# Two middle token blocks turned by DMA, and query halves in the last block pair, in a two-layer spectral and attention kernel

## The chip, the cores and the metric

The kernel runs on one core of a Trainium2 chip. The metric is the device time of one launch in microseconds. The engines are named as in the profile: PE (matmul), ACT (ScalarE), DVE (VectorE), POOL (GpSimd) and SP, whose queue issues nearly all DMAs.

## The reference, cut

x is one sequence of 2048 tokens of 512 elements in bfloat16. Two layers follow each other. Each is a spectral mixing A (a 2-D FFT of the normalized x, multiplied by complex weights, and the inverse) and an attention B with 32 query heads of 16 elements that share one key and one value head, each added to x.

```
def _A_ref(x, w_r, w_i):
    X = rfft2(x, axes=(-2, -1)) * (w_r + 1j * w_i)
    return irfft2(X, s=(S, D), axes=(-2, -1))
def _B_ref(x, wq, wk, wv, wo):
    q, k, v = heads(x @ wq), x @ wk, x @ wv
    p = softmax(q @ k.T * Dh ** -0.5)
    return merge(p @ v) @ wo
x = x + _A_ref(_layernorm(x), w_r, w_i)
x = x + _B_ref(_layernorm(x), wq, wk, wv, wo)
# and both once more
```

## The kernel before, in words

**Tiles.** Token rows are kept as x_sb with four blocks t of four tiles r, 128 rows each. t is also the attention's query block (512 queries). The rows of one block lie with stride 4 in the sequence, so that the FFT over tokens splits into a radix-4 step (`radix4`, L66 to L76), matmuls with tables, and the same again on the way back.

**Stages of a layer.** The front: statistics (`bn`), a transpose of x (`tr_x` on PE, or `turn_x` by way of DRAM), a matmul with the cosine and sine table PH (`mm1`, L1162), scaling by the reciprocal deviation on ACT (`mm1_evac`, L1175), radix-4 on DVE. The middle: matmuls with the tables FT (`mid`), the multiplication by the weights on DVE (`filt`, L1233 to L1236). The back, one block t after the other: inverse matmuls (`inv`), radix-4, `y_mm`, the addition to x (`add_x`, L1317), statistics, `rstd` on ACT, `shift` (L1108) and `apply` (L1115) on DVE, which make the normalized rows xnt; these are transposed on PE (`tr_n`, L1323) and copied to xT (`trn_evac`, L1326, the tile named gx) by ACT or DVE. From xT come K (`k_mm`, L1340), V (`v_mm`, L1352) and Q (`qt_mm`, L1366).

**Attention.** There are 32 blocks b per layer: query block qb, group g of eight heads, and parity par. A block has 64 units of work, 16 key chunks for four heads. One unit is a score matmul of 32 rows (L1382), an exponential, and a matmul with V (L1404). The exponential is made either on ACT (two units at a time, L1387) or on DVE: one operation turns scores into bfloat16 bits (`p1`, L1394), and two additions of constants give two further phases (`phase`, L1398 on POOL or L1400 on DVE), whose mean approximates the exponential. A finished block is transposed out of PSUM (`evac`, L1411); every second block closes a pair: `recip`, `mul`, and a turn by way of DRAM (`norm_dma`), or, for the last pair of a layer, a DVE transpose (`norm`, L1431). Then come the projections (`proj`, L1447), the addition to x and the front of the next layer.

**The order.** Nothing is scheduled at run time. A planner in the kernel file (`Plan`) goes through a modelled time and emits instructions one by one; each engine then runs its own list in order, and waits on semaphores. The planner has a duration for each task, a latency between engines, PSUM slots (four banks b, two double banks sa), and for what goes by DMA an assumed delay: `TURN` (7000 ns) and `OUT_TURN` (25000 ns). SCRIPT is a string of positions at which the planner doesn't take its best choice but the second one, pauses PE, or gives the phase additions to the other engine. DVE units begin (`dve_on`) when V of all four blocks is there; up to then only ACT makes exponentials. Dummy matmuls keep PE's clock up.

```
    def turn_x(self, L, tiles):
        (t, r), _ = tiles
        way = self.way.tile([2 * P, D], BF, name="way")
        self.nc.sync.dma_start(out=way.rearrange("(r p) d -> p r d", r=2), in_=self.x[:, r:r + 2, t, :])
        self.turned(L, tiles, way)
```

Of the kernel before, what the change touches and what calls it, by code (L numbers as in the profile page):

```python
# [10 lines left out]
P = 128  # L11
# [7 lines left out]
NC = 4  # L19
# [70 lines left out]
def phase_weights():  # L90
# [4 lines left out]
RANKS = ((), ())  # L95
TURNS = ("PE", "ACT", "DVE", "POOL", "wait", "few", "heads", "phase")
SCRIPT = (
    "0ax00902q00k05h0hw0po0c807l04j03c00801i00a00p0740ay04w00p01v0vn01903p0790l900i01f0630fk00q01202z0ad09i01h07k0h8"
    "08t0ib00a02g04s0bp08300c02q05k05101200q02300s00903n0960b202107m0ac07h00e00e01e0dc03g0by04r0500bx0rl00g0q803f06u"
    "03d03s02t00a01c08001401711p01q05g00j0ex0iy00t01a03807p05t08200k07409503o00g00x00g03914a00804107x04k01m0310ix00s"  # L100
    "02400u0rv02g05707s09a08805q02o03u02206s0mg03l01k02o03u01t00c04w07401m01l01o09s0d90w50ak0240ng09e03407500p00w00c"
    "06o06d08t03h02l0650c81380aq04o04u01h03f00r08i0190dc0bh11p0ud0e404z02103c01l01n02502s05k09906903f01y00x016018083"
    "03h00y02w02l01x06j0hy00o00r0at01q00z00w05n06m0lt05e00c05k0fx0i00740200m40560fx0mh01i00h04402000d00x02j07102x00k"
    "0b201101l0fc04t06q00p01101y0ls00m04w00i05n01x00j00902803m00s03m02u00l01808y0ba0a50z80wa00s0hw08o02c0ml084")


def script():

    out, n = {}, 0
    for i in range(0, len(SCRIPT), 3):  # L110
        v = int(SCRIPT[i:i + 3], 36)
        n += v // 8
        out.setdefault(n, []).append(TURNS[v % 8])
    return out


class Task:
# [5 lines left out]
    def __init__(self, eng, dur, deps, fn, take=None, give=(), then=None, prio=-1, order=0, lazy=0.0, gap=0.0, parts=1, port=False, lock=False, cols=None):  # L123
        self.ways = {eng: dur} if isinstance(eng, str) else dict(zip(eng, dur))
        self.eng, self.deps, self.fn = next(iter(self.ways)), deps, fn
        self.dur = self.ways[self.eng]
        self.take, self.give, self.then = take, give, then
        self.port, self.lock = port, lock
        self.cols = self.dur * 512.0 / 220.0 if cols is None else cols
        self.prio, self.order, self.lazy, self.gap, self.parts, self.step = prio, order, lazy, gap, parts, 0  # L130
        self.end = self.slot = None


class Plan:
# [34 lines left out]
    OUT_TURN = 25000.0  # L169
# [3 lines left out]
    def __init__(self):  # L173
        self.t = {"PE": 0.0, "ACT": 0.0, "DVE": 0.0, "POOL": 0.0}
# [18 lines left out]
        self.ranks, self.base = None, 0  # L193

    def ranked(self, which):

        self.ranks, self.base = RANKS[which], self.n

    def add(self, *a, **kw):
# [3 lines left out]
        if self.ranks is not None and k.order < 30:  # L203
            i = k.seq - self.base
            if i < len(self.ranks):
                k.prio, k.order, k.lazy = -1, self.ranks[i] / 32, 0.0
# [17 lines left out]
    def step(self):  # L224
        while True:
# [13 lines left out]
            self.turns.discard(eng)  # L239
            return  # L240
# [36 lines left out]
    def bg_next(self, eng):  # L277
        best = None
        for k in self.bg[eng]:
            if any(d.end is None for d in k.deps):  # L280
                continue
            if eng == "ACT" and len(k.ways) > 1 and self.at is not None and self.at.dve_on:
                continue
# [106 lines left out]
    def usable(self, kind):  # L390
# [9 lines left out]
        else:  # L400
            sd, free = (sum(1 for x in self.use if x == y) for y in ("sd", None))
            if not free or sd >= 3 or not at.dve_on and (sd >= self.EARLY_SD or free < 2 or not at.begun or us[0][1] // 4 not in at.v_ready):
                return False
# [3 lines left out]
        return at.unit_ready(us[0]) is not None  # L407

# [87 lines left out]
    def fill(self, start, after):  # L496
# [3 lines left out]
        while self.activity(start) < warm:  # L500
# [8 lines left out]
            else:  # L509
                return  # L510
            if start - t0 < self.MM + (self.PE_SW if mode != after else 0.0) and self.activity(start) >= force:
                return
# [3 lines left out]
            self.t["PE"] = t0 + self.MM  # L516
            if fresh:
                self.bank[i] = t0 + self.MM
# [115 lines left out]
class Attn:  # L634


    def __init__(self, plan, em, layer):
        self.plan, self.em, self.layer = plan, em, layer
        self.blocks = [(qb, g, par) for qb in range(NQB) for g in range(4) for par in range(2)]
        nb = len(self.blocks)  # L640
        first = [(b, 4 * t + r) for t in range(4) for b in range(layer.NFIRST) for r in range(4)]
# [53 lines left out]
    def unit_ready(self, u):  # L695
        b, kc, h = u
        qb, g, par = self.blocks[b]
        if (g, qb) not in self.qt_ready or (kc // 4, par) not in self.k_ready:
            return None
        return max(self.qt_ready[(g, qb)], self.k_ready[(kc // 4, par)])  # L700
# [10 lines left out]
    def done(self, b, slot, end):  # L711
# [5 lines left out]
        self.evac[b] = self.evac_last = ev  # L717
        if par == 0:
            return
        tail = 0.0 if b >= len(self.blocks) - 2 else 5000.0  # L720
        rc = p.add("DVE", 260.0, [ev, self.evac[b - 1]], lambda k: em.recip(self, b), lazy=tail)
        mu = p.add("DVE", 600.0, [rc], lambda k: em.mul(self, b), lazy=tail, port=True)
        if b < len(self.blocks) - 2:
            no = Mark("DMA", None)

            def turned(k):
                em.norm_dma(self, b)
                no.end = k.end + p.OUT_TURN

            mu.then = turned  # L730
        else:
            no = p.add("DVE", 626.0, [mu], lambda k: em.norm(self, b), lazy=tail)
        self.evac[b] = no
        if g == 3:
            self.layer.close_rows(qb, [self.evac[8 * qb + 2 * i + 1] for i in range(4)])


class Layer:
# [9 lines left out]
    PUTC = True  # L748
    FIRST_PUT = (0,)
    BN = ((4,), (4,), (4,), (2, 2))  # L750
# [16 lines left out]
    def pieces(self, durs, deps, fn, order, lazy=0.0, lock=False):  # L767

        for i, d in enumerate(durs):
            deps = [self.plan.add("DVE", d, deps, lambda k, i=i: fn(i), order=order, lazy=lazy, port=True, lock=lock)]  # L770
        return deps[0]
# [90 lines left out]
    def add_back(self):  # L862
        p, em, at = self.plan, self.em, self.at
        left = [T]
        for t in range(T):
            o = 20 + 10 * t
            cs = []
            for b in range(2):
# [17 lines left out]
                cs.append(self.pieces((332.0, 332.0, 400.0, 400.0), es, lambda i, t=t, b=b: em.radix_v(self, t, b, i), o))  # L886
            w = 2 if t == 0 else R
            te = []
            for j in range(0, R, w):
                key, ks = ("b", t, j), []  # L890
                for i, r in enumerate(range(j, j + w)):
                    put = t in self.FIRST_PUT
                    n = 5 if put else 4
                    y = p.add("PE", 217.0 * n, cs, lambda k, s, t=t, r=r, n=n: em.y_mm(self, t, r, k.slot, s, n), parts=n, take="b",
# [12 lines left out]
                nb = p.add("DVE", 100.0, [rs], lambda k, key=key, w=w: em.shift(self, key, w), order=o + 3)  # L907
                for i, r in enumerate(range(j, j + w)):
                    self.stat[("b", t, r)] = (rs, key, i)
                for a in range(j, j + w, 2):  # L910
                    ap = [p.add("DVE", 323.0, [nb], lambda k, t=t, r=r: em.apply(self, t, r), order=o + 3) for r in (a, a + 1)]
# [30 lines left out]
    def close_rows(self, qb, deps):  # L942
        p, em, at = self.plan, self.em, self.at
        t = qb
        if not self.last and t == T - 1:
            p.ranked(1)
# [9 lines left out]
        for r in range(R):  # L956
            if t == T - 1:
                m = p.add("PE", 660.0, deps[:3] + [self.at.evac_last], lambda k, r=r: em.proj(at, t, r, k.slot, 0, 3), take="b",
                          prio=-2)
                if not self.last and self.PUTC:  # L960
# [14 lines left out]
        w = 2 if t == T - 1 else R  # L975
        for j in range(0, R, w):
            n.add_stats(("f", t, j), [(t, r) for r in range(j, j + w)], rows[j:j + w])
        rows = [r.x if hasattr(r, "put") else r for r in rows]
        for j in range(0, R, 2):
            n.add_front([(t, j), (t, j + 1)], rows[j:j + 2], 1, turned[j // 2] if t < T - 1 else None)  # L980
        if t == T - 1:
# [3 lines left out]
            p.ranks = None  # L985


class Emit:
# [117 lines left out]
    def shift(self, L, key, n):  # L1106
        mv, sb = L.sb[key]
        self.nc.vector.scalar_tensor_tensor(out=sb[:, 1, :], in0=mv[:, :, 0], scalar=-1.0, in1=sb[:, 0, :],  # L1108
                                            op0=ALU.mult, op1=ALU.mult)

    def apply(self, L, t, r):
        xn = self.pool.tile([P, 512], BF, name="xnt", tag="xnt", bufs=6)
        _, key, i = L.stat[("b", t, r)]
        sb = L.sb[key][1]
        self.nc.vector.tensor_scalar(out=xn, in0=self.x[:, r, t, :], scalar1=sb[:, 0, i:i + 1], scalar2=sb[:, 1, i:i + 1],  # L1115
                                     op0=ALU.mult, op1=ALU.add)
        L.xn[(t, r)] = xn

    def load_x(self, L):
        for t in range(T):  # L1120
# [8 lines left out]
    def turn_x(self, L, tiles):  # L1129

        (t, r), _ = tiles
        way = self.way.tile([2 * P, D], BF, name="way")
        self.nc.sync.dma_start(out=way.rearrange("(r p) d -> p r d", r=2), in_=self.x[:, r:r + 2, t, :])
        self.turned(L, tiles, way)

# [183 lines left out]
    def tr_n(self, L, t, j, slot, i):  # L1319
        ps = self.ps(slot).bitcast(BF).rearrange("p (c i x) -> p c i x", i=2, c=NC)  # L1320
        xn = L.xn.pop((t, j + i))
# [6 lines left out]
    def trn_evac(self, L, t, j, slot, eng):  # L1328
# [3 lines left out]
        ps = self.ps(slot).bitcast(BF).rearrange("p (c x) -> p c x", c=NC)  # L1332
        self.copy(eng, xT[t][:, :, j:j + 2, :].rearrange("p c i x -> p c (i x)"), ps)
# [42 lines left out]
    def scores(self, at, slot, us):  # L1376
        for j, (b, kc, h) in enumerate(us):
# [3 lines left out]
            o = self.ps(slot)[:, j, :] if slot[0] == "sa" else self.ps(slot)  # L1381
            self.nc.tensor.matmul(o, lhsT=KX[rs, kc * P:(kc + 1) * P], rhs=at.QT[qb][rs, g, :], start=True, stop=True,  # L1382
# [24 lines left out]
    def evac(self, at, b, slot):  # L1407
        qb, g, par = at.blocks[b]
        if par == 0:
            at.raw[(qb, g)] = self.pool.tile([P, 2, 16, 32], F32, name="raw", tag="raw", bufs=3)  # L1410
        self.nc.vector.transpose(out=at.raw[(qb, g)][:, par].rearrange("p a b -> p (a b)"), in_=self.ps(slot))  # L1411

    def recip(self, at, b):
        qb, g, par = at.blocks[b]
        at.rc[(qb, g)] = self.small([2, 16], "rc", 2)
        self.nc.vector.reciprocal(out=at.rc[(qb, g)], in_=at.raw[(qb, g)][:, :, :, 16])

    def mul(self, at, b):
        qb, g, par = at.blocks[b]
        raw, rc = at.raw[(qb, g)], at.rc.pop((qb, g))  # L1420
# [5 lines left out]
    def norm(self, at, b):  # L1426
        qb, g, par = at.blocks[b]
        on = at.raw.pop((qb, g))
        if g == 0:
            at.OT[qb] = self.t4([4, 512])  # L1430
        self.nc.vector.transpose(out=at.OT[qb][:, g, :], in_=on.rearrange("p a h d -> p (a h d)"))  # L1431
# [24 lines left out]
def schedule(plan, em, n_pairs=2):  # L1456
# [5 lines left out]
    plan.ranked(0)  # L1462
    for t in range(T):
        arrive = Mark("DMA", 5500.0 + 2600.0 * t)
        tiles = [(t, r) for r in range(R)]
        j = 0
        for n in L.BN[t]:
            L.add_stats(("f", t, j), tiles[j:j + n], [arrive] * n)
            j += n
        for j in range(0, R, 2):  # L1470
            L.add_front(tiles[j:j + 2], [arrive], 1)
# [4 lines left out]
    plan.ranks = None  # L1476
# [61 lines left out]
```

The softmax here doesn't subtract the row's maximum and nothing guards it: scores larger than these inputs give would overflow.

## Time and profile before

| what | value |
|---|---|
| time, median of 3 runs | 1314.85 us (1314.13 to 1315.22) |
| the profiled execution | 1314.55 us, span 1312.7 us |
| DMA queue of SP and ACT | 108288 packets, 30.46 MB, 10.0% of the span |
| granted PE clock | 1.00 |
| ACT: one exponential of 128x1024 | 1.00 to 1.35 us |
| POOL: one phase addition | 1.04 us |

The page shows one execution. A busy time is the union of an engine's instructions; neighbours overlap by about a tenth of a microsecond, so that the spacing of two starts is a better price than the duration. The idle time in brackets in a timeline is that of the engine ahead of an instruction, with the instruction that ended it.

### The profile page before, as it was taken

What the parts mean: (1) busy time and instruction counts of PE and PEld (TensorE: products, weight loads), DVE (VectorE), ACT (ScalarE), POOL (GpSimd) and SP (SyncE); (2) the same over time, 40 slices, a digit from 0 to 9 for tenths busy, and PEclk for the clock granted to TensorE, in tenths of its full rate; (3) what the DMA queues carried; (4) which work ended last, traced back from release to release, by engine and by line L of the source; (5) the groups of instructions that cost most, each with busy time, mean ns of one, the idle gap of its engine ahead of it and who ended that gap; (6) DMA issues with size and microseconds to landing.
All of it is one profiled execution on the core that took longest, in us unless ns stands there. A gap on an engine that the chain in (4) does not pass through costs nothing.

```text
span 1312.7 us, 31767 instructions
## 1 busy us (share of the span) xinstructions
PE 1281.5 (98%) x12986; PEld 433.1 (33%) x12986; DVE 1272.7 (97%) x2277; ACT 1223.3 (93%) x1397; POOL 840.1 (64%) x825
## 2 busy tenths in 40 slices
PE   9999999999999999999999999999999999999997
PEld 5642222322232222222256423232222232233222
DVE  6999999999999999999979999999999999999998
ACT  6488999999999999999954899999999999999996
POOL 0005777767777677766720067787777777777775
PEclk9999999999999999999999999999999999999999
DMA  9100000011010100010051000000100010000101
GB/s 294 46 1 1 10 9 10 9 32 19 2 12 12 36 10 10 9 34 17 10 169 41 1 1 9 10 10 9 22 14 10 9 22 14 5 8 11 27 5 25
DMA packets 108722, 33.04 MB, mean 25 GB/s; under 512 B 88352, under 2 KB 107296, under 8 KB 108576
## 3 DMA queue, kind: packets, MB, share of 16 engines
q1 hardware_dynamic: 108288, 30.46, 10.0%
q8 instruction: 101, 1.65, 0.5%
q10 hardware_dynamic: 288, 0.56, 0.1%
q14 instruction: 45, 0.37, 0.1%
HBM read 17.89 MB, written 7.60 MB: 19 GB/s over the span
## 4 chain that ended last, share of the span: by engine, by line
ACT 72%; PE 18%; DVE 10%; issue 1%; DVEq 0%
ACT e_0_84 L1387 3%; ACT e_10_94 L1387 3%; ACT e_13_97 L1387 3%; ACT e_3_87 L1387 3%; ACT e_20_104 L1387 3%; ACT e_4_88 L1387 3%; ACT e_12_96 L1387 3%; ACT e_2_86 L1387 3%; ACT e_8_92 L1387 3%; ACT e_7_91 L1387 3%; ACT e_11_95 L1387 3%; ACT e_18_102 L1387 3%; ACT e_1_85 L1387 3%; ACT e_5_89 L1387 3%; ACT e_15_99 L1387 3%; ACT e_14_98 L1387 3%
## 5 line engine op out<-in xcount | busy, mean ns | idle before, releaser
L1382 PEld LDWEIGHTS <-KB 32*128 32x128 bf16 x2048 | 89.7, 91 | 228.5 <-issue 221.4
L1382 PEld LDWEIGHTS <-KA 32*128 32x128 bf16 x2048 | 86.4, 91 | 238.4 <-issue 231.5
L1404 PEld LDWEIGHTS <-vs_116 128*32 128x32 bf16 x2474 | 99.9, 94 | 93.0 <-issue 87.9
L1404 PEld LDWEIGHTS <-vs_117 128*32 128x32 bf16 x1622 | 96.0, 94 | 64.0 <-issue 60.5
L1404 PEld LDWEIGHTS <-vs_118 128*32 128x32 bf16 x1622 | 70.6, 94 | 70.5 <-issue 65.9
L1404 PEld LDWEIGHTS <-vs_119 128*32 128x32 bf16 x1622 | 68.4, 94 | 64.8 <-issue 61.4
L1398 POOL INT64_ADD w_1382<-w_1381 x1 | 1.0, 1040 | 108.1 <-DVE w_1381 L1394 108.1
L1398 POOL INT64_ADD w_10977<-w_10976 x1 | 1.0, 1038 | 97.2 <-DVE w_10976 L1394 97.2
L1387 ACT ACTIVATE e_6_90<-sa_64 128x1024 bf16<-128x1024 f32 x34 | 39.8, 1172 | 1.0 <-PE sa_65 L1382 1.0
L1091 DVE BATCH_NORM_STATS2 st<-x_sb 128x6 f32<-128x512 bf16 x52 | 35.4, 682 | 4.0 <-DMA x_sb<-in_A_x_dram 3.6
L1387 ACT ACTIVATE e_11_95<-sa_65 128x1024 bf16<-128x1024 f32 x31 | 36.5, 1178 | 0.7 <-PE sa_65 L1382 0.7
L1387 ACT ACTIVATE e_12_96<-sa_65 128x1024 bf16<-128x1024 f32 x31 | 36.9, 1189 | 0.2 <-PE sa_65 L1382 0.2
L1387 ACT ACTIVATE e_2_86<-sa_64 128x1024 bf16<-128x1024 f32 x31 | 36.5, 1178 | 0.4 <-PE sa_64 L1382 0.4
L1387 ACT ACTIVATE e_4_88<-sa_65 128x1024 bf16<-128x1024 f32 x31 | 36.6, 1182 | 0.1
L1387 ACT ACTIVATE e_1_85<-sa_64 128x1024 bf16<-128x1024 f32 x31 | 36.6, 1180 | 0.1
L1387 ACT ACTIVATE e_7_91<-sa_64 128x1024 bf16<-128x1024 f32 x31 | 36.6, 1181 | 0.0
L1387 ACT ACTIVATE e_15_99<-sa_65 128x1024 bf16<-128x1024 f32 x31 | 36.6, 1179 | 0.0
L1387 ACT ACTIVATE e_20_104<-sa_65 128x1024 bf16<-128x1024 f32 x31 | 36.4, 1175 | 0.0
L1387 ACT ACTIVATE e_13_97<-sa_64 128x1024 bf16<-128x1024 f32 x31 | 36.2, 1168 | 0.0
L1387 ACT ACTIVATE e_14_98<-sa_65 128x1024 bf16<-128x1024 f32 x31 | 36.0, 1162 | 0.0
L1387 ACT ACTIVATE e_0_84<-sa_65 128x1024 bf16<-128x1024 f32 x30 | 35.5, 1183 | 0.2 <-PE sa_65 L1382 0.2
L1387 ACT ACTIVATE e_9_93<-sa_64 128x1024 bf16<-128x1024 f32 x30 | 35.1, 1170 | 0.2 <-PE sa_64 L1382 0.2
(4077 smaller groups left out, 6474.8 us busy)
## 6 DMA issues: line engine op xcount, KB each, us to landing
it<-const_IT SPq DMA_DIRECT2D x8, 640.0 KB, 5.6
onw<-on SPq DMA_DIRECT2D x120, 32.0 KB, 1.9
x_sb<-in_A_x_dram SPq DMA_DIRECT2D x4, 512.0 KB, 6.8
out_dram<-x_sb SPq DMA_DIRECT2D x16, 128.0 KB, 1.9
way<-x_sb SPq DMA_DIRECT2D x6, 256.0 KB, 2.2
tab_PH<-const_PH ACTq DMA_DIRECT2D x1, 512.0 KB, 4.9
w_131<-const_FT SPq DMA_DIRECT2D x1, 512.0 KB, 8.8
w_136<-const_FT SPq DMA_DIRECT2D x1, 512.0 KB, 8.4
```

The lines of the kernel that those rows point to most:

```text
L1091: self.nc.vector.bn_stats(st, self.ps(slot) if slot else self.x[:, x[1], x[0], :])
L1382: self.nc.tensor.matmul(o, lhsT=KX[rs, kc * P:(kc + 1) * P], rhs=at.QT[qb][rs, g, :], start=True, stop=True, skip_group_check=True)
L1387: self.wrote("ACT", e, self.nc.scalar.activation(out=e, in_=self.ps(slot), func=ACT.Exp, scale=SCALE))
L1398: self.nc.gpsimd.int64_add(t[p][:, 0:n].bitcast(U64), t[0][:, 0:n].bitcast(U64), DELTA[p] * FOUR)
L1404: self.nc.tensor.matmul(self.ps(slot)[32 * h:32 * h + 32, :], lhsT=V[:, kc, :], rhs=rhs, start=first, stop=last, skip_group_check=True)
```

## The change

It does five things in one edit.

1. **Turn by DMA.** The normalized rows of the blocks t = 1 and 2 go to DRAM in two DMAs per pair of tiles, and come back by a DMA transpose into xT (`turn_n`). The transposes on PE and their evacuations fall away for these blocks. For t = 0 and 3 they stay, in the row order 0, 2, 1, 3.
2. **Query halves.** In each layer the last two blocks (b = 30 and 31) no longer stand for the two parities of 512 queries, but for the two halves of the queries, both parities each. Either half is closed by itself (`recip`, `mul`, `norm` at half size, then the projections of two row tiles).
3. **`shift` falls away**: `apply` subtracts the mean and multiplies by the reciprocal deviation. `y_mm` waits for the part of radix-4 that makes its row only.
4. **The start.** x of block 0 arrives in two DMAs, and the planner reckons with a slow PE clock in the first 4.4 us.
5. **The planner.** A new SCRIPT with one more kind of entry, `OUT_TURN` 9000 instead of 25000, the early close of the first half marked urgent.

```
+    DMA_T = (1, 2)
...
-    OUT_TURN = 25000.0
+    COLD = 4400.0
+    OUT_TURN = 9000.0
...
+        self.halves = {nb - 2: 0, nb - 1: 1}
...
+        if b in self.halves:
+            rc = p.add("DVE", 125.0, [ev], lambda k: em.recip(self, b))
+            mu = p.add("DVE", 335.0, [rc], lambda k: em.mul(self, b), port=True)
+            no = p.add("DVE", 340.0, [mu], lambda k: em.norm(self, b))
+            hf = self.halves[b]
+            self.layer.close_rows(qb, [self.evac[8 * qb + 2 * i + 1] for i in range(3)] + [no], (2 * hf, 2 * hf + 1))
+            return
...
-                nb = p.add("DVE", 100.0, [rs], lambda k, key=key, w=w: em.shift(self, key, w), order=o + 3)
...
+                for a in rows[::2]:
+                    d = 1 if t in self.DMA_T else 2
+                    ap = [p.add("DVE", 323.0, [rs], lambda k, t=t, r=r: em.apply(self, t, r), order=o + 3) for r in (a, a + d)]
+                    if d == 1:
+                        te.append(Mark("DMA", None))
+
+                        def applied(k, t=t, a=a, y=te[-1], ap=ap):
+                            if all(z.end is not None for z in ap):
+                                em.turn_n(self, t, a)
+                                y.end = k.end + p.TURN
+                        ap[0].then = ap[1].then = applied
+                        continue
...
+        for j in (0, 2):
+            self.nc.sync.dma_start(out=self.x[:, j:j + 2, 0], in_=self.xv[:, j:j + 2, 0])
+        for t in range(1, T):
...
+    def turn_n(self, L, t, a):
+
+        if t not in L.at.xT:
+            L.at.xT[t] = self.t4([NC, R, P], tag="gx", bufs=4)
+        way = self.way.tile([2 * P, D], BF, name="way", tag="way")
+        for i in range(2):
+            self.nc.sync.dma_start(out=way[P * i:P * i + P, :], in_=L.xn.pop((t, a + i)))
+        out = L.at.xT[t].rearrange("p c r x -> p c (r x)")[:, :, P * a:P * a + 2 * P]
+        self.nc.sync.dma_start_transpose(out=out, in_=way)
...
+            if b in at.halves:
+                q = 256 * at.halves[b]
+                for i, KX in enumerate((self.KA, self.KB)):
+                    self.nc.tensor.matmul(o[:, 256 * i:256 * i + 256], lhsT=KX[rs, kc * P:(kc + 1) * P],
+                                          rhs=at.QT[qb][rs, g, q:q + 256], start=True, stop=True, skip_group_check=True)
+                continue
```

The numbers of the exponentials made on ACT (1237) and of the p1 operations (1622) are the same in both programs. The phase additions on DVE grow from 3 to 9, those on POOL fall from 809 to 803.

## The prediction

> **What bounds the kernel now.** I read the page's busy shares first, then busy time by stage, then the timeline of VectorE (DVE) where a stage begins or ends.
>
> ```profile
> PE 1281.5 (98%) x12986; PEld 433.1 (33%) x12986; DVE 1272.7 (97%) x2277; ACT 1223.3 (93%) x1397; POOL 840.1 (64%) x825
> ```
>
> DVE lacks 40 us of the span, ACT 89. PE's 98% says little, as its ends are modelled and it holds dummy matmuls. The stages are: front and back of layer 1 up to the first DVE-made exponential, attention 1, the same for layer 2, and the tail (columns: stretch, length, busy time and instructions of PE, PEld, DVE, ACT, POOL, clock, DMA):
>
> ```profile
> 0.00:108.10 108.10, 103.33 (x777) 57.88 (x777) 92.66 (x230) 70.40 (x108) 2.36 (x10) 1.00 0.33 104
> 108.10:664.00 555.90, 548.13 (x5754) 162.67 (x5756) 552.52 (x941) 554.91 (x615) 414.63 (x408) 1.00 0.09 17
> 664.00:759.00 95.00, 89.92 (x704) 51.06 (x697) 80.61 (x195) 55.61 (x85) 0.87 (x1) 1.00 0.18 57
> 759.00:1301.30 542.30, 534.91 (x5726) 159.62 (x5726) 540.40 (x903) 541.50 (x592) 421.16 (x406) 1.00 0.07 12
> 1301.30:1312.74 11.44, 5.24 (x40) 1.85 (x32) 6.54 (x9) 0.86 (x1) 1.04 (x1) 1.00 0.14 47
> ```
>
> In both attentions ACT and DVE are full together (idle 1.0 and 3.4 us, then 0.8 and 1.9). Between them (the ramps) DVE is idle for 15.4 and 14.4 us, ACT for 38 and 39. So DVE is the account to keep: span = DVE work + DVE idle, 1272.7 + 40.0. Work moved on DVE saves nothing; only work removed, or idle time closed, does. The idle time is at the stage edges. The one between the layers:
>
> ```profile
> 664.02 1.12 DVE L1400 TENSOR_SCALAR w_9869<-w_9868 128x1024 uint16<-128x1024 uint16 x1
> 665.07 0.42 DVE L1400 TENSOR_SCALAR w_9870<-w_9868 128x1024 uint16<-128x1024 uint16 x1
> 666.18 0.72 DVE L1411 STREAM_TRANSPOSE raw<-b_69 128x512 f32<-128x512 f32 x1 [0.70 <-PE b_69 L1404]
> ...
> 669.75 0.70 DVE L1091 BATCH_NORM_STATS2 st<-b_67 128x6 f32<-128x512 f32 x1 [0.99 <-PE b_67 L1310]
> ...
> 679.24 0.69 DVE L66 TENSOR_TENSOR w_10050<-w_10015 128x1024 bf16<-128x1024 bf16 x1 [3.55 <-ACT w_10015 L1175]
> ```
>
> With 0.93, 0.32 and a 2.83 us wait at 684.71 these make 9.3 us: attention's last block is closed, projected, normalized and transformed as one chain. Other rows used: DVE starts at 4.77 (3.62 us for x), and after its last addition it is idle for 3.3 us of output DMA.
>
> **What the Trainium skill says.** "SBUF — State Buffer" (§ SBUF: two separate sides) calls the port pair of DVE and GpSimd an exclusive lock, held for the whole instruction. The first two lines above agree: the same operation took 1.12 us while a GpSimd addition (663.83 to 664.87) ran, 0.42 after it. "DMA: Bandwidth & Descriptors" (§ Anatomy of one DMA) puts the fixed part of a DMA near 2.0 us and says that waits on semaphores are made by the issuing sequencer. The trace agrees with both: 2.2 us for 256 KB here, and SP stands between copy and transpose:
>
> ```profile
> 279.19 0.39 SPq L1133 DMA_DIRECT2D way<-x_sb  x1
> 281.43 1.27 SPq L1126 DMA_TRANSPOSE e_17_101<-way  x1
> ```
>
> "TensorE: Matmul & The Clock Gate" (§ Part 4: PE-mode transpose) says that transposes don't count as busy for the clock gate; no row here shows it, but it bears on the start.
>
> **The change part by part**, on DVE start to start (an instruction overlaps the next by about 0.09 us). Counts come from the instruction order of both programs.
>
> *Turning token blocks 1 and 2 by DMA.* 64 transposes leave PE, and eight evacuations leave DVE (ACT keeps its four):
>
> ```profile
> 67.81 0.68 DVE L1326 COPY gx<-b_69 128x1024 bf16<-128x1024 bf16 x1
> 68.41 0.28 DVE L70 TENSOR_TENSOR w_866<-e_4_88 128x256 bf16<-128x256 bf16 x1
> ```
>
> 8 x 0.60 = -4.8. The ten shifts (0.13 to 0.17 us, some 0.08 start to start) go: -0.8. The turned rows come later. Per pair, SP issues two copies of 128 KB and a transpose that waits for them. With 0.39 us to issue a copy, 1.9 to land (the output's 128 KB), 1.27 to issue a transpose and 3.2 to land (the rows of x), counted from the end of the first pair's second apply: copies landed at 2.05, transpose issued 2.15 to 3.4, landed 5.35. The second pair's copies stand behind that transpose on SP: issued 3.45 to 4.3, landed 5.8 to 6.2, transpose landed 9.1 to 9.5. The planner counts 7.0 us after the second pair's apply, 7.7 on this scale. In the new order DVE has 7.6 to 8.4 us of work between that apply and the point where PE comes to the K projection (L1340 before): two applies 0.7, radix pieces 1.5 to 3.0, four additions 2.4, three statistics 2.4, at t = 1 a copy 0.6. So PE waits about 1.2 us there. Behind that wait in PE's queue are V, scores and later inverse matmuls; ACT waits for the scores, DVE for K's and V's evacuations, behind which its next applies stand. One statistic (0.8) is still to do on DVE meanwhile. Bounds: 0 if DVE comes that late anyway, 2.0 if nothing overlaps; I take 0.55 each, four places: +2.2 (0 to 8). Other SP work isn't delayed: the inverse tables are issued before, the outputs' turns much later.
>
> *More phase additions on DVE* (L1400), six, that POOL had. 2048 elements took 1.57 us beside POOL (at 1301.39); without it 0.42 x 2 less an overlap, some 0.7. In the new order five stand where POOL has nothing started: 5 x 0.7 + 1.5 = +5.0 (4.0 to 9.4). POOL has 36% to spare.
>
> *Query halves.* Block 30 does both parities of queries 0 to 255, block 31 the rest. Reciprocal, multiply and transpose (0.39 + 0.73 + 0.76) come twice at half size; between half and whole price each, +0.2 per layer, +0.4. PE gets 256 more score matmuls of 256 columns for 256 fewer of 512, which I cost as streaming the same, and 256 more weight loads of 32 rows (KB: 89.7 us for 2048, 0.044 each, 11 us in all) in the shadow of other strips and of PE's waits for ACT and DVE: +0.3 (0 to 3). What it closes: in the new order the first half's two row tiles are projected earlier, though the second of them only at the end of attention, where its statistic fills the 0.70 wait. After the norm remain two tiles instead of four: 8 matmuls of L1162 (1.7 us) and two ACT evacuations (1.4) less ahead of 679.24. I redo the chain with these rows and come to radix at 675.7 and the filter at 680.5 instead of 684.71: 4.2 shorter. But 1.9 of that is DVE work moved ahead into a full attention (half of reciprocal, multiply, norm 0.95; a statistic 0.8; rest 0.15). Idle closed: -2.3 (-4 to -1). In the tail, one addition fills the 0.91 us before the last block's evacuation: -0.6 (-1 to 0).
>
> *The start.* x of block 0 in two DMAs, six dummies instead of 17 ahead of the first transposes, which stood at 7.01 though x was there at 4.77. The next matmuls need tab_PH (issued at 1.19, 4.9 to land: 6.1), and PE may still be slow then. ACT has 20 us of work up to 27.8 with hardly a gap, so an earlier start carries through: -1.5 (-2.5 to 0).
>
> *ACT fits*: the ramps hold 22 exponentials each instead of 25 and 26, so each attention has some four more at 0.91, +3.6, about what DVE gets there. The rest (fewer waits of projections, new order) I cost at nothing, since both engines are full in attention already: 1.0 and 0.8 us of ACT's idle time bound it.
>
> Sum: -4.8 - 0.8 + 2.2 + 5.0 + 0.4 + 0.3 - 2.3 - 0.6 - 1.5 = -2.1 on the span of 1312.7. That execution took 1314.55, the median of the others is 1314.85; so about 1312.7.
>
> **Rivals.** *A, the turn is free*: the transposes land before PE asks, and no addition on DVE meets POOL. Then -2.1 - 2.2 - 1.0 - 0.7 (start and transition at their better side) = -6, some 1309. For it: DVE's 8 us cover most of the flight. Against it: the second pair waits on SP behind the first.
> *B, the turn blocks the ramps*: PE, in order, stands at K of blocks 1 and 2 in both layers until the second transpose has landed. At 2.0 us each, +5.8 above my sum, and with additions meeting POOL another +1.5: -2.1 + 7.3 = +5, some 1320. It decides from about 1.1 us of DVE wait per place (4 x 0.55 more than counted). For it: no slack in either queue. Against it: statistics left to do.
> *C, a wash*: the six additions on DVE cost what the eight evacuations gave, and the start changes nothing because the tables come late: within 2 us of 1314.85.
>
> **How the numbers follow.** Forecast 0.45, A 0.22, B 0.26, C 0.07. A measurement can tell about 0.2%, 2.6 us, from no change. The forecast's own range, 1309 to 1316, lies half below 1312.2, four tenths within, one tenth above. Faster: 0.22 + 0.22 + 0.01 (C) = 0.45; slower: 0.05 + 0.23 (B) = 0.28; same: 0.27. The range takes A's better end (start and transition at their bounds, 1305.5) and B with its cost at the bound (1321).
>
> **What would show it.** In the page after: DVE work within 3 us of 1272.7, ten L1108 rows gone, L1326's copies of gx on DVE 4 instead of 12. In the waits of PE: K's weight loads behind a transpose, with the us per place. In the timeline: radix of block 3 in layer 2 some 12 us after the last exponential of DVE instead of 15.3; first ACT copy before 6. It is wrong if DVE's idle time in the ramps falls by more than 8 us, or if attention, at the counts above, grows by over 7 us in either layer.

## The result, and the profile after

The changed kernel takes 1322.42 us (1321.17 to 1324.77, four runs) beside 1314.70 for the kernel before in the same comparison: ratio 1.0061, 95% interval 1.0043 to 1.0078. It is slower, and 1.4 us beyond the range given. The profiled execution has a span of 1320.5 us, 7.8 above that of before.

The busy line of the page:

```profile
PE 1281.0 (97%) x13168; PEld 432.4 (33%) x13168; DVE 1272.1 (96%) x2271; ACT 1224.4 (93%) x1397; POOL 837.1 (63%) x819
```

VectorE's (DVE's) work is 0.6 us less than before; its idle time went from 40.0 to 48.4. By stage, cut as before (columns: stretch, length, busy time and instructions of PE, PEld, DVE, ACT, POOL, granted clock, DMA share, GB/s):

```profile
0.00:109.42 109.42, 98.22 (x726) 54.44 (x727) 90.39 (x222) 67.61 (x105) 2.36 (x10) 0.98 0.41 121
109.42:672.50 563.08, 554.86 (x5899) 164.93 (x5899) 556.52 (x950) 559.42 (x619) 413.05 (x404) 0.99 0.09 17
672.50:765.27 92.77, 86.48 (x649) 48.55 (x646) 76.34 (x185) 51.36 (x81) 0.96 (x1) 0.98 0.27 80
765.27:1311.60 546.33, 537.85 (x5869) 163.38 (x5868) 543.50 (x909) 545.97 (x595) 419.71 (x404) 1.00 0.07 12
1311.60:1320.50 8.90, 3.59 (x29) 1.06 (x28) 5.30 (x8) 0.05 (x1) 1.04 (x1) 0.90 0.13 44
```

Against before: first ramp +1.3, attention 1 +7.2, second ramp -2.2, attention 2 +4.0, tail -2.5. Two things stand out. DVE is idle for 19.0 us in the first ramp, where it was 15.4, though it has less to do there. And the clock, 1.00 in every stage before, is below it in four stages (the tail's fall also comes with the copies first, 0.97, so that one is not the turn's).

The first shows on SyncE's queue. Token block 2 of layer 1, in its timeline:

```profile
88.91 0.81 SPq L1164 DMA_DIRECT2D way<-xnt  x2
91.16 1.23 SPq L1166 DMA_TRANSPOSE gx<-way  x1
92.44 1.04 SPq L1164 DMA_DIRECT2D way<-xnt  x2
96.22 1.23 SPq L1166 DMA_TRANSPOSE gx<-way  x1
```

The first pair's copies are followed by its transpose at 91.16. Only then are the second pair's copies issued, 3.5 us after the first ones, although all four rows had been normalized by 89.86. They take 2.7 us from the end of their issue to the second transpose; at the other three places it is 1.4 to 1.5. PE's timeline around it:

```profile
96.06 0.39 PE L1420 MATMUL sa_65<-w_887,KA 32*128 32x512 bf16 x2
...
99.51 1.38 PE L1372 MATMUL b_68<-gx,wk_81 128*128 128x512 bf16 x4 [2.51 <-DMA gx<-way]
...
101.67 0.61 PE L1420 MATMUL sa_64<-w_887,KA 32*128 32x512 bf16 x2 [0.37 <-ACT KA L1378]
```

PE stands at the K projection for 2.51 us until the second transpose lands, 10.6 us after the first copies were issued. After the wait two score matmuls of the same form take 0.61 us instead of 0.39. And DVE, whose last row had ended at 98.57:

```profile
101.65 0.75 DVE L1380 TENSOR_SCALAR KB<-b_68,part 128x512 bf16<-128x512 f32 x1 [3.07 <-ACT KA L1378]
```

The bracket names ACT's KA, the last of several waits; ACT itself had waited 3.4 us for K. At block 1 the same gap is 1.75 us. In layer 2 it is 1.81 at block 1 and 0.44 at block 2, with one of 1.48 between them at the next addition of x (0.45 with the copies first, below).

The transition, on DVE, did what was forecast:

```profile
678.38 0.70 DVE L1116 BATCH_NORM_STATS2 st<-b_67 128x6 f32<-128x512 f32 x1 [0.81 <-PE b_67 L1342]
...
684.50 0.69 DVE L66 TENSOR_TENSOR w_10148<-w_10094 128x1024 bf16<-128x1024 bf16 x1 [2.79 <-ACT w_10094 L1207]
```

The radix of block 3 comes 12.0 us after the last DVE-made exponential (672.50), where it was 15.3.

### The profile page after: what moved, and what is told of

It reads as the page before. It is cut to its first block, busy times and chain, and to the rows that moved or that the text cites. A ratio compares the mean times of both kernels' runs of the same rounds, so it can differ in the third digit from the quotient of the medians.

```text
span 1320.5 us, 32179 instructions
## 1 busy us (share of the span) xinstructions
PE 1281.0 (97%) x13168; PEld 432.4 (33%) x13168; DVE 1272.1 (96%) x2271; ACT 1224.4 (93%) x1397; POOL 837.1 (63%) x819
## 4 chain that ended last, share of the span: by engine, by line
ACT 65%; PE 21%; DVE 10%; DMA 2%; issue 1%; SPq 0%; DVEq 0%
ACT e_5_89 L1425 3%; ACT e_4_88 L1425 3%; ACT e_2_86 L1425 3%; ACT e_15_99 L1425 3%; ACT e_6_90 L1425 3%; ACT e_9_93 L1425 3%; ACT e_1_85 L1425 3%; ACT e_19_103 L1425 3%; ACT e_8_92 L1425 3%; ACT e_12_96 L1425 3%; ACT e_7_91 L1425 3%; ACT e_11_95 L1425 3%; ACT e_3_87 L1425 3%; ACT e_14_98 L1425 3%; ACT e_17_101 L1425 3%; ACT e_0_84 L1425 3%
## 5 line engine op out<-in xcount | busy, mean ns | idle before, releaser
L1420 PEld LDWEIGHTS <-KA 32*128 32x128 bf16 x1920 | 82.9, 91 | 227.6 <-issue 220.3
L1420 PEld LDWEIGHTS <-KB 32*128 32x128 bf16 x1920 | 84.2, 91 | 215.0 <-issue 208.0
L1442 PEld LDWEIGHTS <-vs_116 128*32 128x32 bf16 x2474 | 98.2, 94 | 89.7 <-issue 85.5
L1425 ACT ACTIVATE e_2_86<-sa_64 128x1024 bf16<-128x1024 f32 x31 | 35.8, 1155 | 2.0 <-PE b_68 L1420 1.6
L1425 ACT ACTIVATE e_14_98<-sa_65 128x1024 bf16<-128x1024 f32 x31 | 36.4, 1175 | 0.8 <-PE sa_65 L1420 0.8
L1425 ACT ACTIVATE e_11_95<-sa_64 128x1024 bf16<-128x1024 f32 x32 | 36.9, 1153 | 0.1
L1425 ACT ACTIVATE e_9_93<-sa_65 128x1024 bf16<-128x1024 f32 x32 | 36.9, 1154 | 0.0
L1425 ACT ACTIVATE e_19_103<-sa_64 128x1024 bf16<-128x1024 f32 x31 | 36.0, 1162 | 0.9 <-PE sa_65 L1420 0.9
L1425 ACT ACTIVATE e_13_97<-sa_65 128x1024 bf16<-128x1024 f32 x31 | 35.7, 1151 | 1.0 <-PE sa_64 L1420 1.0
L1425 ACT ACTIVATE e_5_89<-sa_64 128x1024 bf16<-128x1024 f32 x30 | 35.2, 1173 | 1.0 <-PE sa_65 L1420 1.0
L1425 ACT ACTIVATE e_12_96<-sa_64 128x1024 bf16<-128x1024 f32 x30 | 35.8, 1193 | 0.3 <-PE sa_64 L1420 0.3
L1425 ACT ACTIVATE e_6_90<-sa_65 128x1024 bf16<-128x1024 f32 x30 | 35.6, 1185 | 0.3 <-PE sa_65 L1420 0.2
L1425 ACT ACTIVATE e_17_101<-sa_64 128x1024 bf16<-128x1024 f32 x31 | 35.9, 1157 | 0.0
L1425 ACT ACTIVATE e_7_91<-sa_64 128x1024 bf16<-128x1024 f32 x30 | 35.4, 1181 | 0.2 <-PE sa_64 L1420 0.2
L1425 ACT ACTIVATE e_8_92<-sa_65 128x1024 bf16<-128x1024 f32 x30 | 35.0, 1166 | 0.5 <-PE sa_64 L1420 0.3
L1425 ACT ACTIVATE e_1_85<-sa_64 128x1024 bf16<-128x1024 f32 x30 | 34.8, 1160 | 0.7 <-PE sa_64 L1420 0.7
```

What stands on the lines that cost most here:

```text
L1425: self.wrote("ACT", e, self.nc.scalar.activation(out=e, in_=self.ps(slot), func=ACT.Exp, scale=SCALE))
L1442: self.nc.tensor.matmul(self.ps(slot)[32 * h:32 * h + 32, :], lhsT=V[:, kc, :], rhs=rhs, start=first, stop=last, skip_group_check=True)
```

## The experiments

Theory T: the late second transpose costs twice, by PE's wait in both ramps and by a half clock that the wait brings on. Rival A (of this section, not the prediction's A): the price is the six additions (L1400 before) that moved to DVE. Each kernel is the changed one except where another is named; none leaves computation out.

**Copies first.** Both pairs' copies are issued before both transposes; each engine's own order stays.

```
-        self.nc.sync.dma_start_transpose(out=out, in_=way)
+        self.late = getattr(self, "late", []) + [(out, way)]
+        if len(self.late) == 2:
+            for out, way in self.late:
+                self.nc.sync.dma_start_transpose(out=out, in_=way)
+            self.late = []
```

> Only SP's order changes: both pairs of a block are copied to DRAM before the first transpose is issued, so the second transpose should land about 6.7 us after the first pair's apply instead of 9.5 to 10.5. Theory T (the turn lands late, PE stands at K, and its clock falls to half in the 3 to 7 us that follow): DVE's idle time before K's evacuation of blocks 1 and 2 falls from 1.8, 3.1, 1.8 and 1.9 us to under 0.5 each, the half-speed stretches at 100, 110 and 745 us go, and the time falls by 7 to 11 us, to 1312 to 1316. Rival A (attention's new order and the phase additions on DVE cost the 8 us): the time falls by less than 4 us, to above 1318.

Measured: 1312.53 us (1310.89 to 1314.43), ratio to before 0.9984 (0.9977 to 0.9990): 9.9 us under the changed kernel, and faster than both. SyncE's queue, same block:

```profile
88.92 1.81 SPq L1164 DMA_DIRECT2D way<-xnt  x4
91.20 2.58 SPq L1169 DMA_TRANSPOSE gx<-way  x2
```

The second transpose is issued by 93.78 instead of 97.45. The stages:

```profile
0.00:105.88 105.88, 98.95 (x726) 55.33 (x727) 90.31 (x221) 67.79 (x105) 2.35 (x10) 1.00 0.43 125
105.88:666.14 560.26, 552.09 (x5899) 164.61 (x5899) 556.28 (x950) 559.23 (x619) 413.03 (x404) 1.00 0.09 17
666.14:755.57 89.43, 84.97 (x649) 48.66 (x646) 76.24 (x185) 51.29 (x81) 0.96 (x1) 1.00 0.28 82
755.57:1301.88 546.31, 537.78 (x5869) 163.00 (x5868) 543.49 (x909) 545.95 (x595) 419.69 (x404) 1.00 0.07 12
```

The clock is back at 1.00 in these four. K no longer waits for its rows, and DVE no longer for K at block 2 of layer 1:

```profile
96.93 1.04 PE L1376 MATMUL b<-gx,wk 128*128 128x512 bf16 x4
98.73 0.75 DVE L1384 TENSOR_SCALAR KB<-b,part 128x512 bf16<-128x512 f32 x1
```

Against the changed kernel: first ramp -3.5, attention 1 -2.8, second ramp -3.3, attention 2 and tail 0.0. So the late turn cost 9.7 us of span between these two executions. (The changed kernel's had the earlier front by 1.6 us, see the run on x of block 0 below; from the same instruction on, its first ramp is 5.1 us longer.) What is left of the change against before is -2.2, +4.4, -5.6, +4.0, -2.5: -1.9.

**Ten dummy matmuls, then five**, ahead of the K projection of blocks 1 and 2, to keep PE busy over the wait (the second kernel has range(5)):

```
+        if c == 0 and t in L.DMA_T:
+            for _ in range(10):
+                self.nc.tensor.matmul(self.ps(slot), lhsT=self.zero[:, 0:128], rhs=self.zero,
+                                      start=True, stop=True, skip_group_check=True)
```

> Ten dummy matmuls of 512 columns (2.2 us at full clock) stand right ahead of K of blocks 1 and 2, so PE is busy while the turn is in flight; the transposes land as late as before. Theory T: the wait for rows stays in DVE's idle time (some 7 us in all), but the half-speed stretches go, 3 us of DVE's idle time after 110 us and part of the stretch at 745 us with them: 3 to 5 us faster than the changed kernel, 1317 to 1319. If the clock is no part of it: no faster, and slower by up to 3 us where the dummies outlast the flight. Rival A: no difference, within 1 us.

> The changed kernel, with five dummy matmuls in PE's queue ahead of the K projection of blocks 1 and 2 (ten had made it longer). Theory T (the late second transpose costs twice: PE's wait, and then a half clock that the wait brings on): five dummies end about when the transpose lands, so the waits before K's evacuation stay under 2.5 us, the clock stays at 1.00 in the first ramp and in the first 10 us of attention 1, and the time is 1 to 4 us under the changed kernel's, 1318 to 1321. Rival (only the wait itself costs; the clock has no part): no gain, 1322 to 1325. In both, the time stays 6 us or more above the kernel with the copies first (1312.5), since the transpose still lands late.

Ten: 1324.98 us (1323.23 to 1327.64), ratio 1.0082 (1.0070 to 1.0095). A miss: at two of the four places they outlast the flight (K follows them without a wait), at the other two PE still waits 0.71 and 0.90 us for the transpose. DVE's waits before K's evacuation, total and times, in the first ramp (4.8, twice, in the changed kernel):

```profile
DVE KB L1383 <- ACT KA L1381: 5.7, 3, 3.2
```

Five: 1319.68 us (1317.94 to 1320.18), ratio 1.0036 (1.0023 to 1.0048), within the expectation. Its first three stages:

```profile
0.00:109.08 109.08, 100.63 (x726) 56.27 (x737) 90.31 (x221) 67.78 (x105) 2.35 (x10) 1.00 0.41 122
109.08:669.34 560.26, 548.55 (x5870) 164.34 (x5899) 556.28 (x950) 559.22 (x619) 413.02 (x404) 1.00 0.09 17
669.34:762.11 92.77, 86.60 (x648) 49.35 (x656) 76.35 (x184) 51.29 (x81) 0.95 (x1) 1.00 0.28 80
```

This parts the two costs in attention. Attention 1 is 560.26, to the hundredth that of the copies-first kernel: the 2.8 us there were the clock. The ramps stay long, though K stands for only 0.31 and 0.48 us behind the dummies in layer 1: the second is 92.77 as in the changed kernel, the first, from the same instruction on (the first L58 after 27 us), 76.1 us long, for 77.9 in the changed kernel and 72.8 with the copies first. What the half clock takes inside the ramps is not parted: of the 1.9 us between 77.9 and 76.1, some 1.3 can be the second pair's copies at block 2, which here took 1.5 us from the end of their issue to the transpose, and 2.7 there, in the same order on SyncE's queue. In slices of 2 us the changed kernel had

```profile
110.00:112.00 2.00, 2.00 (x6) 0.49 (x6) 1.30 (x3) 1.70 (x2) 0.00 (x0) 0.58 0.03 8
112.00:114.00 2.00, 2.00 (x12) 0.27 (x14) 0.72 (x3) 0.66 (x1) 0.00 (x0) 0.50 0.00 0
114.00:116.00 2.00, 2.00 (x17) 0.32 (x9) 1.39 (x4) 1.27 (x2) 1.84 (x2) 0.50 0.00 0
```

where ACT and DVE, full in attention otherwise, starve beside a PE that shows as busy throughout; with five dummies the clock is 1.00 in each of these. Over all runs its mean clock is 0.998 to 1.00, the changed kernel's 0.994 to 0.997.

**The additions on POOL**, alone, and together with the copies first:

```
-        self.em.phase(t, p, len(us), eng)
+        self.em.phase(t, p, len(us), "POOL" if self.at.peek("DVE") or self.p1_fifo else eng)
```

> The six phase additions that the new order gives to DVE inside attention are emitted on POOL at the same place; all other orders are the same. Rival A: DVE loses 5.0 us of work (as I priced it, 4.0 to 9.4) and the time falls by 4 to 5 us, to about 1318. Theory T: attention runs at the pace of ACT and DVE together, whose shares are fixed, so at most 1 to 3 us come back, and POOL's later results may cost as much.

> Both edits together: copies of both pairs ahead of the transposes, and the six additions on POOL. Theory T: as the first run, within 2 us of it (1311 to 1316). Rival A: as the run with the additions on POOL alone, within 2 us of it.

Alone: 1324.53 us (1324.29 to 1327.98), ratio 1.0085 (1.0071 to 1.0098), no faster than the changed kernel, with a mean clock of 0.992 to 0.995. With the copies first: 1312.56 us (1310.39 to 1313.70), ratio 0.9984 (0.9977 to 0.9990), as without. Its attentions:

```profile
106.57:666.85 560.28, 552.00 (x5899) 164.52 (x5899) 554.55 (x946) 559.24 (x619) 416.87 (x408) 1.00 0.09 17
...
756.26:1302.05 545.79, 537.25 (x5869) 162.85 (x5868) 542.16 (x907) 545.56 (x595) 420.94 (x406) 1.00 0.07 12
```

DVE has 1.7 and 1.3 us less to do, and the stages are as long within 0.5 us (560.28 for 560.26, 545.79 for 546.31). Rival A falls.

**x of block 0 in one DMA again**, in the copies-first kernel:

```
-        for j in (0, 2):
-            self.nc.sync.dma_start(out=self.x[:, j:j + 2, 0], in_=self.xv[:, j:j + 2, 0])
-        for t in range(1, T):
+        for t in range(T):
```

> The kernel with the copies first, with x of block 0 loaded by one DMA of 512 KB again instead of two. If the prediction's term for the start (-1.5) stands: 1314.0, and the first ramp 1.5 us longer than in the kernel with the copies first (105.9). If the start gains nothing, because the ramp waits for tables and ACT's chain: within 0.5 us of 1312.5.

Measured: 1312.67 us (1311.02 to 1313.78), ratio 0.9984 (0.9978 to 0.9991), 0.1 above the copies-first kernel; the first ramp is 106.2 for 105.9. The second DMA for x is worth nothing that can be told by the medians. The rest of the start (six dummies for 17, the planner's order) this run doesn't test, and the start differs between executions. The same instruction of DVE in the kernel before, the changed kernel and the copies-first kernel:

```profile
33.35 1.29 DVE L58 TENSOR_TENSOR w_487<-w_444 128x1024 bf16<-128x1024 bf16 x2 [2.90 <-ACT w_444 L1216]
31.48 1.29 DVE L58 TENSOR_TENSOR w_474<-w_431 128x1024 bf16<-128x1024 bf16 x2 [2.90 <-ACT w_431 L1248]
33.08 1.29 DVE L58 TENSOR_TENSOR w<-w 128x1024 bf16<-128x1024 bf16 x2 [2.90 <-ACT w L1252]
```

In the changed kernel's profiled execution the first sixteen matmuls with PH take 3.6 us (6.86 to 10.49), in that of the copies-first kernel 4.9 (7.20 to 12.08), and the front comes 1.6 us later. The 21 times of the copies-first kernel lie apart in the same way, 7 at 1310.9 to 1311.1 and 14 at 1312.4 to 1314.4; that this is the start isn't shown, since only one of them has a profile.

**Without the lists.** The rollout list (SCRIPT) is emptied in the kernel before, in the copies-first kernel (twice, the second time beside the next two), and in two versions of the latter: one turns all middle blocks on PE (DMA_T empty), one closes the last block pair as before. The planner's own rules then order everything, so these compare structures, each in the order that its planner gives it (between the kernel before and the others `OUT_TURN` and the smaller changes differ too). The last edit is shown without the lines that restore the old close.

```
-SCRIPT = (
...
+SCRIPT = ""
...
-    DMA_T = (1, 2)
+    DMA_T = ()
...
-        self.halves = {nb - 2: 0, nb - 1: 1}
+        self.halves = {}
```

> The kernel before with the list of rollout decisions emptied, so that the planner orders everything by its own rules. The yardstick for the three kernels run with it; by itself it says what the list was worth: 0.5 to 2.5% slower than the kernel before, 1321 to 1348, if the list is worth what such a search usually finds.

> The kernel with the copies first, its list emptied too. Theory T (the structure itself gains some 2 us: halves and the evacuations, less four exponentials more on ACT in each attention): 1 to 6 us under the emptied kernel before. Rival (the gain of the kernel with the copies first comes from its new list alone): no faster than the emptied kernel before.

> The emptied kernel with the copies first once more, as the yardstick on the chip on which the next two run: within 0.3% of its other run.

> The emptied kernel with the copies first, with all four middle blocks turned on PE again (64 transposes and eight more evacuations on DVE or ACT), halves kept. Theory T (in the ramps DVE's evacuations are worth their 4.8 us, and with the copies first the flight costs nothing): 2 to 6 us slower than with the DMA turn, most of it in the two ramps. Rival (the DMA turn is worth nothing even with the copies first, because the transpose still lands late): within 1.5 us, or faster.

> The emptied kernel with the copies first, with the last block pair closed as in the kernel before (a parity in each block, all 512 queries), DMA turn kept. Theory T (halves shorten the transition by some 3 us and the tail by some 2.5, and cost attention little): 3 to 6 us slower than with halves. Rival (what the transition gains is work moved ahead into attention, which gets longer by as much): within 1.5 us.

| lists emptied | us | ratio to the kernel before, interval |
|---|---|---|
| before | 1332.62 | 1.0137 (1.0123 to 1.0150) |
| copies first | 1323.80 | 1.0069 (1.0056 to 1.0081) |
| copies first, again | 1323.41 | 1.0068 (1.0055 to 1.0080) |
| with PE's turn | 1329.47 | 1.0115 (1.0101 to 1.0129) |
| without halves | 1326.80 | 1.0095 (1.0079 to 1.0110) |

The structure gains 9 us: within it the DMA turn is worth 6.1 and the halves 3.4, if the second run of the middle kernel is the yardstick; the rest of the change was not taken apart. The turn's part was expected mostly in the ramps: they give 2.0 of the 6.8 us of span, attention 1 gives 3.5, a miss, and why is open, since the planner's order differs too. The halves' part is where it was expected: second ramp 1.7, tail 1.7. The old list was worth 1332.6 - 1314.6 = 18.0 us to its kernel, the new one 1323.6 - 1312.5 = 11.1. So, if the two worths simply add, 7 of the 9 us go again with the exchange of lists; what is left is the 2 of the copies-first kernel.

**Work priced at 3.6 us on ACT, or on DVE**, in each attention of the copies-first kernel. The doubled instruction writes the same values again; four exponentials at 0.91 in the first kernel, six p1 at 0.60 in the second:

```
+        if self.nexp % 627 in (150, 250, 350, 450):
+            self.nc.scalar.activation(out=e, in_=self.ps(slot), func=ACT.Exp, scale=SCALE)
...
+        for _ in range(2 if self.np1 % 818 in (150, 275, 400, 525, 650, 775) else 1):
```

> The kernel with the copies first, with four exponentials of each attention done twice on ACT (same input, same output): 4 x 0.91 = 3.6 us more ACT work in each attention. Theory T (ACT alone sets the length of attention): each attention longer by 3.0 to 3.7, in all 1312.5 + 6 to 7.4 = 1318.5 to 1320. Rival (DVE is the account, as the prediction had it): at most 1.0 and 0.4 us of ACT's idle time are used up first and DVE's own row is unchanged, so under +3 in all if ACT had hidden room, 1313 to 1315.5.

> The kernel with the copies first, with six of DVE's first-phase exponentials of each attention done twice on DVE (same input, same output): 6 x 0.60 = 3.6 us more DVE work in each attention, which is as much as the other kernel puts on ACT. Theory T (DVE has 4.0 and 2.8 us of room there, ACT none): under 2 us in all, 1312.5 to 1314.5. Rival (DVE is the account): each attention longer by 3 or more, in all 1318.5 to 1320, as on ACT.

On ACT: 1321.16 us (1319.29 to 1322.57), ratio 1.0052 (1.0038 to 1.0066), 8.6 over the copies-first kernel, somewhat more than the upper bound of either theory. On DVE: 1318.46 us (1316.62 to 1320.29), ratio 1.0030 (1.0019 to 1.0042), 5.9 over it. Attention 1 of the first, then of the second kernel:

```profile
105.82:670.30 564.48, 552.28 (x5899) 164.91 (x5899) 557.09 (x950) 563.32 (x623) 413.76 (x404) 1.00 0.09 17
```

```profile
105.96:669.10 563.14, 554.48 (x5899) 163.92 (x5899) 559.32 (x956) 560.53 (x619) 413.74 (x404) 1.00 0.09 17
```

From 560.26, ACT's work lengthens it by 4.2 and DVE's by 2.9 (attention 2: by 4.1 and 2.8). The two pieces of work were not equal, though: ACT's busy time grew by 4.1 in attention 1 (559.23 to 563.32) and 4.0 in attention 2, DVE's by 3.0 (556.28 to 559.32) and 3.4. So ACT's work shows in full, and 0.95 and 0.8 of DVE's. Theory T said under 1 us for DVE, so "ACT alone" falls as well: both engines set the length.

## Why the prediction was wrong, step by step

**The step that failed: "So PE waits about 1.2 us there ... I take 0.55 each, four places: +2.2."** The late turn cost 9.9 us (the copies-first kernel beside the changed one). The place and the mechanism were named (PE stands at K, and the second pair's copies stand behind the first transpose on SP), and PE's wait itself was sized nearly right. Beside the 2.51 above:

```profile
85.49 1.04 PE L1372 MATMUL b_67<-gx,wk_81 128*128 128x512 bf16 x4 [1.42 <-DMA gx<-way]
743.61 1.02 PE L1372 MATMUL b_67<-gx,wk_81 128*128 128x512 bf16 x4 [1.83 <-DVE mv L1117]
756.33 1.02 PE L1372 MATMUL b_67<-gx,wk_81 128*128 128x512 bf16 x4 [0.34 <-DMA gx<-way]
```

That is 1.5 us on average for 1.2. (At 743.61 the bracket names a statistic of DVE; the transpose had been issued 3.4 us earlier, as at the other places.) What failed is DVE's share of it, 0.55, and what came after:

- What follows the landing. K's matmuls and ACT's KA stand between the landing and DVE: 1.8 us from K's start to KB, 2.1 at block 2 of layer 1. The sum left them out. DVE had more left when PE began to wait than the "one statistic", 1.5 to 1.8 us, but that only made up for K and KA, so nearly all of PE's wait came through: 1.75, 3.07, 1.81 and 0.44 us before KB. In the copies-first kernel the 1.8 us at block 2 are filled with statistics. Together DVE's idle time is 3.5 and 3.2 us more per ramp than with the copies first, 1.7 for each of four places instead of 0.55, and 2.1 if the first ramp is counted from the same instruction on. Part of this is half clock inside the ramps.
- The flight. From the end of the first pair's second apply to K it took some 9.2, 10.3, 9.2 and 9.0 us, where 9.1 to 9.5 was reckoned. The outlier is block 2 of layer 1, with the 2.7 us of its second copies; why they were slow there is open.
- The clock: 2.8 us in attention 1 (five dummies), foreseen nowhere. The Trainium skill, "TensorE: Matmul & The Clock Gate" (§ Part 1), says that the array falls to half rate after about 3.4 us of idle window and that the window runs free. The page was read for the start, not for the wait that the change adds.

The prediction's rival B had this mechanism with 2.0 us per place and 1320. It measured 1.7 to 2.1 per place; B's total also held 1.5 for additions that meet POOL, and lacked the clock. What spoke against it, "statistics left to do", was the wrong estimate: they cover K and KA, not the wait.

**The additions, "5 x 0.7 + 1.5 = +5.0"**: five last 0.68 us and one 1.23, about as priced. Six fewer on DVE take 3.05 us off its work (1271.6 to 1268.6), and nothing off the time. Why is not settled. They may stand where DVE would wait anyway, or POOL's slower addition (1.05 us mean, 1.40 for the larger ones) may come as much later for PE. DVE's idle time in attention grows by what its work shrinks in either case. A kernel that tells them apart was not tried.

**"Work moved on DVE saves nothing"; DVE is the account.** The sum of DVE's work was right: -0.2 forecast, -0.6 in the changed kernel, -1.1 with the copies first. As a price it is half right: work added in attention costs most of its length on DVE (2.9 of the 3.0 us by which its busy time grew), but all of it on ACT too, which the account left out (4.2 of 4.1), and six additions taken off DVE gave nothing. **"ACT fits: ... some four more at 0.91, +3.6, about what DVE gets there"**: three more exponentials each by count (600 for 597, 595 for 592) and one copy, ACT's work +4.3 and +4.5, the attentions +4.4 and +4.0. The growth was foreseen, and DVE's work there grew with it, by 3.8 and 3.1.

**The evacuations, -4.8, and shifts, -0.8**: not measured alone; with the lists emptied and the turn's wait gone, the DMA turn is worth 6.1 us in time, of which the ramps show 2.0.

**The transition, -2.3**: the radix came at 12.0 us (11.8 forecast), and DVE's waits up to the filter fell from 9.3 to 7.6 us (0.29, 0.81, 0.92, 2.79 and 2.83), 1.7 of the 2.3; with the copies first the whole second ramp's idle time fell by 1.2. **The tail, -0.6**: one addition does fill the old gap, and DVE's idle time there fell by 1.3. **The start, -1.5**: ACT's first copy came at 5.07, and the front 1.9 us earlier than before in the changed kernel's profiled execution, but 0.3 in that of the copies-first kernel. The term came true in one and not in the other.

Without the turn's +2.2 the sum was -4.3; the copies-first kernel gives -1.9 of span. By the DVE account its work fell by 1.1 (-0.2 forecast), its idle time by 0.8 (39.2 for 40.0), where the terms for transition, tail and start make 4.4: the first ramp's idle time rose by 0.1, the second's fell by 1.2, the tail's by 1.3, and both attentions' rose by 1.5 together. That the total in time, -2.1, is equal to the forecast is an accident: there it contains a turn's wait, here it doesn't.

**The sign that would prove it wrong** ("attention ... grows by over 7 us in either layer") did come: +7.2 in attention 1, of which 2.8 is the clock; without it the sign would have stayed away (4.4).

## What to carry to other kernels

When a step is handed from an engine to DMA, follow the queue that issues it: a copy queued behind a transpose that itself waits for a copy makes two flights serial. Issuing all copies first cost nothing and turned a loss of 0.6% into a gain of 0.16%. Price a new wait of TensorE by what runs between its end and the engine that counts, and by the clock after it; and when two engines are full together, add work to each, read from its busy time how much it was, and only then price moves between them. Telling the planner a longer `TURN` than 7.0 us was not tried.

## What the runs showed of the hardware

A wait of PE of 2.5 us, less than the 3.4 of the page above, was followed by half clock: 0.52 in the slice from 100 to 102 us after the wait that ended at 99.51, and again 0.50 to 0.58 from 110 to 116. In layer 2 one of 1.83 us was followed by 0.80 and 0.50 (744 to 748), while one of 1.42 at 84 to 85.5 left the clock at 1.00. The stretch at 110 has no long wait right ahead of it; in the five-dummies kernel, with as little PE work from 108 to 110 (1.37 of 2.00 us in both), the clock stayed at 1.00. So that work alone does not decide; whether earlier work does, or where the window happens to lie, was not settled. The mean clock of the changed kernel differs between runs (0.994 or 0.997), as does its time.

Ten dummies instead of five, meant to hold the clock, made the waits longer (5.7 us for 3.8 before KB in the first ramp) and did not hold it (0.73 to 0.50 from 112 to 116).
